# One 512-column matmul for the two parts of the tokens in an MLP's first layer

## The chip, the core and the metric

The kernel runs on one core of one Trainium2 chip. TensorE (PE) multiplies, VectorE (DVE), ScalarE (ACT) and GpSimd (POOL) do the rest, and SyncE (SP) issues most DMAs. The metric is the device time of one execution in microseconds (us). A program is run several times, and the median is compared.

## What is computed

A block of 2048 tokens with 640 channels: a layer norm with shift and scale from a condition, a long convolution with gates, a second layer norm, and an MLP with squared Relu, added to the stream with a gate. The change lies in the MLP:

```python
def _B_ref(x, w1, b1, w2, b2):
    h = jnp.einsum("bsd,df->bsf", x, w1) + b1     # 640 -> 1728
    zero = jnp.zeros_like(h)
    r = jnp.where(h > zero, h, zero)
    h = r * r
    out = jnp.einsum("bsf,fd->bsd", h, w2) + b2   # 1728 -> 640
    return out

h = _layernorm(x, axis=-1) * (1 + cb) + sb
x = x + gb * _B_ref(h, B_w1, B_b1, B_w2, B_b2)
```

## The kernel before

The first half of the time (up to about 290 us) goes to the convolution, which the change does not touch. The MLP follows. It works on eight chunks of `CH` = 256 tokens (`n` = 0 to 7) and, within a chunk, on 14 tiles of the hidden layer (`f` = 0 to 13): thirteen of 128 hidden units and a last one of 64.

Matrices go through PE in the type float32r. To keep the precision, each operand is split in a high part and a low part (the rest): `WI[1, f]` holds both parts of the first layer's weights, `XT[n]` both parts of the chunk's normalized tokens, with shape [128, 2, 5, 256] (part, block of 128 channels, token), and a ring `hring` both parts of the hidden units. A product is then the sum of three: high by high, high by low and low by high.

- `mlp_front(n, f, b)` multiplies block `b` of the five channel blocks. For a full tile these are three matmuls of 256 columns (line 720), all into one PSUM tile `h`; fifteen for the five blocks. The pool of tag "T" gives two such tiles by turns. The tile of 64 units keeps its weights' two parts side by side and has two matmuls for each block (line 711). `mlp_front_first` does the first two tiles of chunk 0 (line 734).
- `mlp_front_end` takes the PSUM tile to SBUF: ACT adds the bias and applies Relu (line 752, tile `mtmp`), POOL squares (line 151, a helper's line). For the tile of 64 units, whose two halves of PSUM hold two sums, it is ACT with the bias (748), VectorE's add (154), ACT's Relu (750) and POOL's square.
- `mlp_split` makes the two parts of the result: ACT copies the high part to `hring` (line 146, a helper's), and VectorE subtracts (line 157).
- `mlp_back(n, f)` is the second layer: 12 matmuls of 320 columns into four PSUM tiles `acc` (line 790), and 8 for the tile of 64 units.
- `mlp_end` multiplies the four sums by the gate on VectorE (line 805), which frees them for the next chunk; `mlp_out` adds the stream, for one half on POOL and for the other on VectorE (line 154), and stores.
- In tiles 8 to 12 of a chunk the next chunk's tokens are made: `prep_xt1` transposes on PE (685) and scales on VectorE (687); `prep_xt2` copies the high part on ACT (146) and subtracts the low part on POOL (157).

The order on each engine is that in which the code is written; `keep_order` pins it. One step `i` of the loop over all (n, f) writes the second layer of the tile three steps back (`MLAG` = 3), the split of the tile one step back, the first layer of this tile, its way out of PSUM, and then what else the step has:

```python
mlp_back(*seq[i - MLAG])       # mlp_end when that was a chunk's last tile
mlp_split(*seq[i - 1])
for b in range(NB):
    mlp_front(*seq[i], b)
mlp_front_end(*seq[i])
```

Of the kernel before, what the change touches and what calls it, by code (L numbers as in the profile page):

```python
# [11 lines left out]
F32 = mybir.dt.float32  # L12
F32R = mybir.dt.float32r
AF = mybir.ActivationFunctionType
ALU = mybir.AluOpType
# [3 lines left out]
P = 128  # L19
NB = D // P  # L20
# [4 lines left out]
CH = 256  # L25
# [67 lines left out]
def ssm_mlp_kernel(  # L93
# [21 lines left out]
    pe, act, dve, pool, sp = nc.tensor, nc.scalar, nc.vector, nc.gpsimd, nc.sync  # L115
# [12 lines left out]
    ps = ctx.enter_context(tc.tile_pool(name="ps", bufs=1, space=bass.MemoryType.PSUM))  # L128
# [21 lines left out]
    def mul(eng, o, a, b):  # L150
        eng.tensor_mul(o, a, b)  # L151

    def add(eng, o, a, b):
        eng.tensor_add(o, a, b)  # L154
# [430 lines left out]
    WI = {}  # L585
# [52 lines left out]
    XT = {}  # L638
# [63 lines left out]
    b1t = sb.tile([P, NF], F32, tag="b1t", name="b1t")  # L702
    accs, hs, rs, hps = {}, {}, {}, {}

    def mlp_front(n, f, b):
        m = P if f < NF - 1 else 64
        if b == 0:
            hps[n, f] = ps.tile([P, CH], F32, tag="T", name=f"h_{n}_{f}", bufs=2)
        if m < P:
            for x in range(2):  # L710
                pe.matmul(  # L711
                    hps[n, f],
                    WI[1, f][:, b],
                    XT[n][:, x, b],
                    start=(b == 0 and x == 0),
                    stop=(b == NB - 1 and x == 1),
                )
            return
        for i, (a, x) in enumerate(((0, 0), (0, 1), (1, 0))):
            pe.matmul(  # L720
                hps[n, f][:m],
                WI[1, f][:, a, b],
                XT[n][:, x, b],
                start=(b == 0 and i == 0),
                stop=(b == NB - 1 and i == 2),
            )
# [15 lines left out]
    def mlp_front_end(n, f):  # L742
        m = P if f < NF - 1 else 64
        r = ML["r"][(n * NF + f) % 3]
        h = hps.pop((n, f))
        if m < P:

            act.activation(r[:m], h[m:], AF.Identity, bias=b1t[:m, f : f + 1])
            add(dve, r[:m], h[:m], r[:m])
            act.activation(r[:m], r[:m], AF.Relu)  # L750
        else:
            act.activation(r[:m], h[:m], AF.Relu, bias=b1t[:m, f : f + 1])  # L752
        mul(pool, r[:m], r[:m], r[:m])
# [463 lines left out]
    for i in range(len(seq) + MLAG):  # L1217
        if i >= MLAG:
            n, f = seq[i - MLAG]
# [7 lines left out]
        if i <= last:  # L1227
            n, f = seq[i]
            if i >= 2:
                for b in range(NB):  # L1230
                    mlp_front(n, f, b)
            mlp_front_end(n, f)
            if n == 0:
                if f >= 8 and f - 8 < NB:
                    prep_xt1(n + 1, f - 8)
                beside(f)
            if n + 1 < NC:
                if f == 3:
                    load_x1(n + 1)
                if n and f == 5:  # L1240
                    stats2(n + 1)
                if n and f == 6:
                    stats2_root(n + 1)
                    stats2_end(n + 1)
                if n == 0 and f in (5, 6):
                    prep_hat(1, f - 5)
                if n and f == 7:
                    prep_hat(n + 1, 0)
                    prep_hat(n + 1, 1)
                if f >= 8 and f - 8 < NB:  # L1250
                    (prep_xt if n else prep_xt2)(n + 1, f - 8)
            if f >= 11 and f < 13:
                residual(n, f - 11, pool)
# [25 lines left out]
```

## Time and profile before

| | us |
|---|---|
| median of 3 runs | 696.17 |
| the three runs | 697.38, 691.37, 696.17 |
| the profiled execution, its own time | 693.38 |
| its span, first to last instruction | 691.6 |

The profiled execution is one more than the three runs. Its span is what the trace covers; the rest of its time lies before the first and after the last instruction. In the trace an engine's row has a line of the kernel (often a helper's), the tile written, an arrow, and the tiles read. "PEld" are the weight loads of PE, which run beside its matmuls.

### The profile page before, as it was taken

What the parts mean: (1) busy time and instruction counts of PE and PEld (TensorE: products, weight loads), DVE (VectorE), ACT (ScalarE), POOL (GpSimd) and SP (SyncE); (2) the same over time, 40 slices, a digit from 0 to 9 for tenths busy, and PEclk for the clock granted to TensorE, in tenths of its full rate; (3) what the DMA queues carried; (4) which work ended last, traced back from release to release, by engine and by line L of the source; (5) the groups of instructions that cost most, each with busy time, mean ns of one, the idle gap of its engine ahead of it and who ended that gap; (6) DMA issues with size and microseconds to landing.
All of it is one profiled execution on the core that took longest, in us unless ns stands there. A gap on an engine that the chain in (4) does not pass through costs nothing.

```text
span 691.6 us, 21100 instructions
## 1 busy us (share of the span) xinstructions
PE 657.0 (95%) x9164; PEld 630.8 (91%) x9164; DVE 335.9 (49%) x601; ACT 330.1 (48%) x688; POOL 311.4 (45%) x390
## 2 busy tenths in 40 slices
PE   6699898889999999999999999999999999999996
PEld 4689798778898888889999999999999999999996
DVE  5267584658886697487532322323332332422313
ACT  4436656767976976466324333333233233233221
POOL 1062165359869789443523514415325325225213
PEclk9999999999999999999999999999999999999999
DMA  9897998889671643466020010100200200200101
GB/s 234 244 270 230 233 265 233 236 204 233 191 221 34 173 148 113 127 199 181 1 77 1 26 52 1 41 37 1 77 1 1 77 1 1 77 1 1 39 1 39
DMA packets 110960, 74.76 MB, mean 108 GB/s; under 512 B 48658, under 2 KB 96146, under 8 KB 110868
## 3 DMA queue, kind: packets, MB, share of 16 engines
q1 hardware_dynamic: 108912, 72.87, 37.2%
q8 instruction: 72, 1.18, 0.7%
q10 hardware_dynamic: 1892, 0.54, 0.4%
q14 instruction: 20, 0.16, 0.1%
q0 software_dynamic: 64, 0.01, 0.0%
HBM read 58.98 MB, written 14.42 MB: 106 GB/s over the span
## 4 chain that ended last, share of the span: by engine, by line
PE 81%; DVE 6%; ACT 5%; DMA 4%; issue 2%; POOL 1%; DVEq 0%; POOLq 0%; ACTq 0%; SPq 0%
PE acc L790 27%; PE h L720 26%; PE qp L464 5%; PE pa L383 4%; PE x L398 4%; PE y L541 4%; PE h L398 3%; DMA wm<-in_w_mod_dram 3%; PE t L530 2%; PE h L711 1%; PE xtp L685 1%; DVE KV L261 1%; ACT wx L146 1%; DVE kacc L261 1%; PE vt L276 1%
## 5 line engine op out<-in xcount | busy, mean ns | idle before, releaser
L151 POOL TENSOR_TENSOR mtmp<-mtmp 128x256 f32<-128x256 f32 x112 | 71.4, 638 | 244.4 <-ACT mtmp L752 236.5
L720 PE MATMUL h<-xt,w_S 128*128 128x256 f32 x1290 | 167.5, 281 | 1.1 <-DVE w_S L157 1.1
L720 PEld LDWEIGHTS h<-xt,w_S 128*128 128x128 f32 x1290 | 161.7, 190 | 1.3 <-DVE w_S L157 1.3
L790 PE MATMUL acc<-w_S,hring 128*128 128x320 f32 x960 | 156.6, 311 | 0.2 <-DVE hring L157 0.2
L157 DVE TENSOR_TENSOR hring<-mtmp,hring 128x256 fp32r<-128x256 f32 x112 | 65.4, 584 | 168.3 <-ACT hring L146 168.3
L790 PEld LDWEIGHTS acc<-w_S,hring 128*128 128x128 f32 x960 | 141.7, 188 | 0.8 <-DVE hring L157 0.7
L752 ACT ACTIVATE mtmp<-h,b1t 128x256 f32<-128x256 f32 x104 | 49.4, 475 | 174.0 <-PE h L720 170.8
L146 ACT ACTIVATE hring<-mtmp 128x256 fp32r<-128x256 f32 x112 | 46.5, 416 | 48.8 <-POOL mtmp L151 47.5
L383 PE MATMUL pa<-wx,p 64*64 64x64 f32 x2560 | 49.3, 228 | 10.8 <-issue 6.1
L383 PEld LDWEIGHTS pa<-wx,p 64*64 64x64 f32 x2560 | 43.9, 141 | 16.8 <-issue 11.3
L146 ACT ACTIVATE a<-pa 128x512 f32<-128x512 f32 x80 | 43.5, 608 | 19.7 <-PE pa L383 19.2
L151 DVE TENSOR_TENSOR wx<-x,wx 128x512 f32<-128x512 f32 x64 | 40.8, 683 | 18.9 <-PE x L398 7.7
L541 PE MATMUL y<-wx,wx 128*64 128x64 f32 x1280 | 43.9, 224 | 2.9 <-ACT wx L146 1.6
L541 PEld LDWEIGHTS y<-wx,wx 128*64 128x64 f32 x1280 | 39.9, 138 | 7.4 <-issue 3.4
L398 PE MATMUL x<-a,gb 128*64 128x128 f32 x640 | 41.6, 274 | 3.3 <-DVE wx L151 2.1
L687 DVE TENSOR_SCALAR we<-xtp,cbs 128x256 f32<-128x256 f32 x35 | 19.0, 543 | 46.8 <-PE xtp L685 46.8
L398 PEld LDWEIGHTS x<-a,gb 128*64 128x64 f32 x640 | 35.9, 137 | 4.9 <-PE h L398 3.0
L154 POOL TENSOR_TENSOR wm<-wm,wm 128x640 f32<-128x640 f32 x20 | 32.1, 1606 | 16.9 <-ACT wm L341 16.5
L261 DVE SCALAR_TENSOR_TENSOR KV<-kt,tap,KV 128x511 f32<-128x511 f32 (+2 forms) x48 | 35.9, 748 | 7.6 <-ACT ktail L146 6.0
L146 ACT ACTIVATE q<-qp 128x512 f32<-128x512 f32 (+1 forms) x40 | 21.3, 584 | 35.4 <-PE qp L464 35.4
L398 PE MATMUL h<-a,gb 128*64 128x128 f32 x512 | 34.0, 275 | 1.5 <-ACT wx L146 1.5
L790 PE MATMUL acc<-w_WX,hring 128*128 128x320 f32 x192 | 31.4, 312 | 0.0
(142 smaller groups left out, 1014.2 us busy)
## 6 DMA issues: line engine op xcount, KB each, us to landing
wm<-in_w_mod_dram SPq DMA_DIRECT2D x25, 320.0 KB, 4.1
KV<-in_A_k_dram SPq DMA_DIRECT2D x20, 256.0 KB, 4.6
KV<-in_A_v_dram SPq DMA_DIRECT2D x20, 256.0 KB, 4.4
p<-in_A_ssm_k_dram SPq DMA_DIRECT2D x20, 256.0 KB, 4.7
p<-kv_d SPq DMA_DIRECT2D x20, 256.0 KB, 4.1
xp<-in_A_q_dram SPq DMA_DIRECT2D x20, 256.0 KB, 4.3
q<-in_A_q_dram SPq DMA_DIRECT2D x15, 320.0 KB, 4.5
out_dram<-x SPq DMA_DIRECT2D x14, 320.0 KB, 2.2
```

What stands on the lines that cost most here:

```text
L146: act.activation(o, i, AF.Copy)
L151: eng.tensor_mul(o, a, b)
L154: eng.tensor_add(o, a, b)
L157: eng.tensor_sub(o, a, b)
L261: dve.scalar_tensor_tensor(o, tk[:, : 512 - t], tap[:, b, t : t + 1], o, op0=ALU.mult, op1=ALU.add)
L383: pe.matmul(t[e][64 * r : 64 * r + 64, g].rearrange("p m d -> p (m d)"), pt[b][l, i, 8 * q + g, :], cw[l, r], start=True, stop=True,)
L398: pe.matmul(t[64 * a : 64 * a + 64, s + r], gb[:, g, r, a], AX[b][i][:, 2 * g + a], start=True, stop=True,)
L464: pe.matmul(t[a][:, u], gi[l, 4 * j + u, r], w[r][l, u % 2], start=(r == 0), stop=(r == 1),)
L541: pe.matmul(y[64 * h : 64 * h + 64, 4 * (g % 2) + i].rearrange("p c l d -> p (c l d)"), tss[g][:, i, 64 * r : 64 * r + 64], ca[:, r, h], s ...
L720: pe.matmul(hps[n, f][:m], WI[1, f][:, a, b], XT[n][:, x, b], start=(b == 0 and i == 0), stop=(b == NB - 1 and i == 2),)
L752: act.activation(r[:m], h[:m], AF.Relu, bias=b1t[:m, f : f + 1])
L790: pe.matmul(acc[2 * s + i], h[:, a, s * P : (s + 1) * P], w[:, y, i * 320 : (i + 1) * 320], start=(f == 0 and ti == 0), stop=(f == NF - 1 ...
```

## The change

For full tiles of chunks 1 to 7, the PSUM tile gets two halves of 256 columns and fills its whole 2 KB per partition. One matmul of 512 columns multiplies the weights' high part with both parts of the tokens, read as two runs of 256 columns that lie 5 x 256 elements apart: high by high goes to half 0, high by low to half 1. A second matmul of 256 columns adds low by high to half 0. For each channel block there are thus two matmuls in place of three. The order within a block is both, low for block 0 and low, both for the others.

Behind it, ACT adds the bias to half 1 as it moves it to SBUF, VectorE adds half 0, and one more VectorE operation takes max(r, 0) and multiplies it by r, which is the squared Relu. POOL's square is gone for these tiles. Chunk 0 and the tiles of 64 units stay as they were.

```diff
     def mlp_front(n, f, b):
         m = P if f < NF - 1 else 64
         if b == 0:
-            hps[n, f] = ps.tile([P, CH], F32, tag="T", name=f"h_{n}_{f}", bufs=2)
+            hps[n, f] = ps.tile(
+                [P, 2, CH] if n and m == P else [P, CH], F32, tag="T", name=f"h_{n}_{f}", bufs=2
+            )
+        if n and m == P:
+
+            h, w = hps[n, f], WI[1, f]
+            both = (h, w[:, 0, b], XT[n][:, :, b])
+            low = (h[:, 0], w[:, 1, b], XT[n][:, 0, b])
+            for x in (both, low) if b == 0 else (low, both):
+                pe.matmul(*x, start=(b == 0 and x is both), stop=(b == NB - 1 and x is both))
+            return
...
+        elif n:
+            act.activation(r, h[:, 1], AF.Identity, bias=b1t[:, f : f + 1])
+            add(dve, r, h[:, 0], r)
+            dve.scalar_tensor_tensor(r, r, 0.0, r, op0=ALU.max, op1=ALU.mult)
+            return
         else:
             act.activation(r[:m], h[:m], AF.Relu, bias=b1t[:m, f : f + 1])
         mul(pool, r[:m], r[:m], r[:m])
```

Lines behind the change have moved: 790 is now 805, and 805 is now 820. The new matmuls are on line 717, the max-times on line 764.

PE's order around the end of chunk 1, before. `h_2_1` is tile 1 of chunk 2, `acc_1_0` to `acc_1_3` are chunk 1's four sums, whose last tile of 64 units comes between two tiles of chunk 2:

```order
L720 MATMUL h_2_1_5964<-xt_2_5728,w_S1_3849 128x256 x15
L790 MATMUL acc_1_0_5517<-w_KV_4901,hring_4976 128x320 x2
L790 MATMUL acc_1_1_5518<-w_KV_4901,hring_4976 128x320 x2
L790 MATMUL acc_1_2_5519<-w_KV_4901,hring_4976 128x320 x2
L790 MATMUL acc_1_3_5520<-w_KV_4901,hring_4976 128x320 x2
L720 MATMUL h_2_2_6000<-xt_2_5728,w_S0_4233 128x256 x15
L790 MATMUL acc_2_0_6018<-w_S1_3849,hring_4976 128x320
```

The second of those fronts and what follows it, on PE, in the changed kernel:

```order
L717 MATMUL h_2_2_5940<-xt_2_5692,w_S0_4233 128x512
L717 MATMUL h_2_2_5940<-xt_2_5692,w_S0_4233 128x256 x2
L717 MATMUL h_2_2_5940<-xt_2_5692,w_S0_4233 128x512
L717 MATMUL h_2_2_5940<-xt_2_5692,w_S0_4233 128x256
L717 MATMUL h_2_2_5940<-xt_2_5692,w_S0_4233 128x512
L717 MATMUL h_2_2_5940<-xt_2_5692,w_S0_4233 128x256
L717 MATMUL h_2_2_5940<-xt_2_5692,w_S0_4233 128x512
L717 MATMUL h_2_2_5940<-xt_2_5692,w_S0_4233 128x256
L717 MATMUL h_2_2_5940<-xt_2_5692,w_S0_4233 128x512
L805 MATMUL acc_2_0_5954<-w_S1_3849,hring_4976 128x320
```

Ten matmuls stand where fifteen stood, and tiles and second layer follow one another as before.

VectorE's order at the same place, before. `hring` is the split, the four rows of line 805 are the products with the gate, and `x1_1` is the stream of chunk 1:

```order
L157 TENSOR_TENSOR hring_4976<-mtmp_4806,hring_4976 64x256
L157 TENSOR_TENSOR hring_4976<-mtmp_4806,hring_4976 128x256
L805 TENSOR_TENSOR mtmp_4806<-acc_1_0_5517,gbrow_4865 128x320
L805 TENSOR_TENSOR mtmp_4806<-acc_1_1_5518,gbrow_4865 128x320
L805 TENSOR_TENSOR mtmp_4806<-acc_1_2_5519,gbrow_4865 128x320
L805 TENSOR_TENSOR mtmp_4806<-acc_1_3_5520,gbrow_4865 128x320
L157 TENSOR_TENSOR hring_4976<-mtmp_4806,hring_4976 128x256
L154 TENSOR_TENSOR x1_1_3020<-mtmp_4806,x1_1_3020 128x640
```

And in the changed kernel:

```order
L157 TENSOR_TENSOR hring_4976<-mtmp_4806,hring_4976 128x256
L154 TENSOR_TENSOR mtmp_4806<-h_2_1_5908,mtmp_4806 128x256
L764 SCALAR_TENSOR_TENSOR mtmp_4806<-mtmp_4806 128x256
L820 TENSOR_TENSOR mtmp_4806<-acc_1_0_5505,gbrow_4865 128x320
L820 TENSOR_TENSOR mtmp_4806<-acc_1_1_5506,gbrow_4865 128x320
L820 TENSOR_TENSOR mtmp_4806<-acc_1_2_5507,gbrow_4865 128x320
L820 TENSOR_TENSOR mtmp_4806<-acc_1_3_5508,gbrow_4865 128x320
L157 TENSOR_TENSOR hring_4976<-mtmp_4806,hring_4976 128x256
L154 TENSOR_TENSOR x1_1_3020<-mtmp_4806,x1_1_3020 128x640
L154 TENSOR_TENSOR mtmp_4806<-h_2_2_5940,mtmp_4806 128x256
L764 SCALAR_TENSOR_TENSOR mtmp_4806<-mtmp_4806 128x256
```

The add and the max-times of tile 1 of chunk 2, which wait for ACT, now stand ahead of the four products of chunk 1, and those of tile 2 stand behind the stream's add.

## The prediction

> **What bounds the kernel now.** I read the page first, for the engine that is busiest, then the busy times by stretch of the span, then the groups by line in the stretch that the change touches, and last the timeline there, which gives the price of one matmul. The page:
>
> ```profile
> span 691.6 us, 21100 instructions
> PE 657.0 (95%) x9164; PEld 630.8 (91%) x9164; DVE 335.9 (49%) x601; ACT 330.1 (48%) x688; POOL 311.4 (45%) x390
> ```
>
> PE is busy for 95% of the span. Busy time by stretch, the columns being PE, PEld, DVE, ACT, POOL, the granted clock, DMA share and GB/s:
>
> ```profile
> 0.00:100.00 100.00, 83.38 (x2020) 75.61 (x2022) 58.31 (x113) 50.27 (x95) 30.64 (x69) 0.98 0.92 244
> 345.00:687.00 342.00, 341.35 (x2607) 341.08 (x2605) 104.41 (x218) 111.40 (x247) 117.28 (x149) 1.00 0.07 26
> 384.10:433.70 49.60, 49.60 (x381) 49.60 (x380) 15.64 (x34) 16.70 (x37) 17.52 (x23) 1.00 0.08 28
> ```
>
> The idle PE time lies at the start, where DMA is busy. The change acts on chunks 1 to 7 of the MLP, which run from about 345 us to the end. There PE is never out of work at full clock, and the other engines are busy for a third of the time. The third row is one chunk. So what a chunk saves on PE comes off the end, as long as the vector work behind it does not become late. The groups of that stretch (after the bar: busy us, mean ns of one; then idle time before it and who ended it):
>
> ```profile
> L720 PE MATMUL h<-xt,w_S 128*128 128x256 f32 x1119 | 145.1, 281 | 0.0
> L790 PE MATMUL acc<-w_S,hring 128*128 128x320 f32 x840 | 136.5, 311 | 0.0
> L151 POOL TENSOR_TENSOR mtmp<-mtmp 128x256 f32<-128x256 f32 x89 | 55.9, 628 | 211.9 <-ACT mtmp L752 211.9
> L157 DVE TENSOR_TENSOR hring<-mtmp,hring 128x256 fp32r<-128x256 f32 x90 | 51.5, 572 | 146.9 <-ACT hring L146 146.9
> L752 ACT ACTIVATE mtmp<-h,b1t 128x256 f32<-128x256 f32 x89 | 42.3, 476 | 160.2 <-PE h L720 160.2
> ```
>
> Neither matmul line idles; ACT, POOL and DVE wait down the chain that starts with PE. The means of 281 and 311 ns are lengths of overlapping instructions and not their spacing. The spacing is in the timeline, start of one row to start of the next, here around the end of chunk 1 and near the end of the kernel (columns: start us, length us, engine, line, tiles, count):
>
> ```profile
> 392.44 1.33 PE L790 MATMUL acc<-w_KV,hring 128*128 128x320 f32 x8
> 392.70 0.48 ACT L752 ACTIVATE mtmp<-h,b1t 128x256 f32<-128x256 f32 x1 [1.92 <-PE h L720]
> 392.93 1.68 DVE L805 TENSOR_TENSOR mtmp<-acc,gbrow 128x320 f32<-128x320 f32 x4 [1.69 <-PE acc L790]
> 393.61 1.95 PE L720 MATMUL h<-xt,w_S 128*128 128x256 f32 x15
> 393.96 1.57 POOL L154 TENSOR_TENSOR x<-mtmp,x 128x640 f32<-128x640 f32 x1
> 394.53 1.28 DVE L157 TENSOR_TENSOR hring<-mtmp,hring 128x256 fp32r<-128x256 f32 x1
> 395.39 1.92 PE L790 MATMUL acc<-w_S,hring 128*128 128x320 f32 x12
> 395.74 0.81 DVE L154 TENSOR_TENSOR x<-mtmp,x 128x640 f32<-128x640 f32 x1
> 397.15 0.27 PE L720 MATMUL h<-xt,w_S 128*128 128x256 f32 x1
> ...
> 680.29 1.36 PE L711 MATMUL h<-xt,w_KV 128*128 128x256 f32 x10
> 681.49 1.93 PE L790 MATMUL acc<-w_WX,hring 128*128 128x320 f32 x12
> ```
>
> Fifteen matmuls of 256 columns take 395.39 - 393.61 = 1.78 us, 118.7 ns each; the ten of L711 take 1.20 us, 120 ns each. Twelve of 320 columns take 397.15 - 395.39 = 1.76 us, 146.7 ns each. From 120 to 146.7 ns is 26.7 ns for 64 columns, 0.417 ns a column. So 256 columns stream for 106.7 ns and 320 for 133.3 ns, and both leave 13.3 ns over: a fixed price for each matmul with its weight load, which is the same for two lengths.
>
> **The change, part by part.**
>
> *Front matmuls.* For each of the 13 full tiles in each of 7 chunks, 91 tiles, fifteen matmuls of 256 columns become five of 512 and five of 256. The columns stay the same: 15 x 256 = 5 x 512 + 5 x 256. Five matmuls and five weight loads go. No row has 512 columns, so it is bounded. From below: columns alone, 512 x 0.417 = 213.3 ns. From above: two of 256 as now, 2 x 118.7 = 237.4 ns. A price above that would need a reason that no row shows, and is a rival below. The line through 256 and 320 columns gives 213.3 + 13.3 = 226.7 ns, which I take because it is nearest to the 320-column row and because the fixed part did not shrink from 256 to 320. Per tile 5 x 13.3 = 66.7 ns go, and 91 x 66.7 ns = 6.1 us. The ends are 91 x 5 x (237.4 - 213.3) ns = 11.0 us saved, and nothing saved. All of it lies on PE, which is the path.
>
> The Trainium skill, page "TensorE: Matmul & The Clock Gate", section "Back-to-back issue gap", gives columns / 2.4 + 2.5 ns for the spacing of warm isolated matmuls. This would make 109 ns of 256 columns and 136 ns of 320, 10 ns under both rows; an estimate by the page for 512 is 215.8 ns, and the sum would be 9.8 us instead of 6.1.
>
> *Bias and Relu on ACT become bias alone.* Both are one pass over 256 columns of PSUM (476 ns, the L752 group above). The first layer's tile of 64 rows has the same bias pass already:
>
> ```profile
> L748 ACT ACTIVATE mtmp<-h,b1t 64x256 f32<-64x256 f32 x7 | 3.3, 474 | 10.8 <-PE h L711 10.8
> L154 DVE TENSOR_TENSOR mtmp<-h,mtmp 64x256 f32<-64x256 f32 x7 | 2.9, 418 | 9.1 <-ACT mtmp L748 9.1
> L261 DVE SCALAR_TENSOR_TENSOR KV<-kt,tap,KV 128x511 f32<-128x511 f32 x16 | 12.0, 748 | 6.4 <-ACT ktail L146 6.0
> ```
>
> So this costs nothing.
>
> *Square on POOL goes, add and max-times on VectorE come.* POOL loses 628 ns a tile (L151 above), off the path. The add is the L154 row, 0.42 us. For the max-times of 256 columns there is no row: its ends are 0.42 us (that same pass) and 0.75 us (the same operation on 511 columns, L261); I take 0.45, since it has the columns of the first. VectorE's busy time in a chunk grows from 15.64 to 15.64 + 13 x 0.87 = 27 us of about 48.7. From ACT's start to the split's end it is 0.48 + 0.42 + 0.45 on the new way against 0.48 + 0.63 on the old, then copy and split as now, so 0.25 us more on a chain that may be late by far: the tile is read by the second layer three tiles later, and two fronts and three backs, 2 x 1.7 + 3 x 1.76 = 8.7 us, lie between, one back less at the last tiles. PE, which covers it, does not run dry. The tile's PSUM buffer comes free after the add instead of after ACT, 0.45 us later, and is wanted again after back, front and back, 5.2 us.
>
> *Who stands behind the new waits on VectorE.* Two things. First, in tiles 8 to 12 the scaling of the next chunk's tokens:
>
> ```profile
> 424.43 0.47 ACT L752 ACTIVATE mtmp<-h,b1t 128x256 f32<-128x256 f32 x1 [2.16 <-PE h L720]
> 424.59 0.54 DVE L687 TENSOR_SCALAR we<-xtp,cbs 128x256 f32<-128x256 f32 x1 [1.68 <-PE xtp L685]
> 425.17 0.42 ACT L146 ACTIVATE xt<-we 128x256 fp32r<-128x256 f32 x1 [0.26 <-DVE we L687]
> 425.66 0.74 POOL L157 TENSOR_TENSOR xt<-we,xt 128x256 fp32r<-128x256 f32 x1
> 426.08 0.60 DVE L157 TENSOR_TENSOR hring<-mtmp,hring 128x256 fp32r<-128x256 f32 x1 [0.94 <-ACT hring L146]
> ```
>
> The scaling now waits for ACT, add and max-times: it starts at 424.43 + 0.47 + 0.42 + 0.45 = 425.8 and not at 424.59, 1.2 us later. Its parts of the tokens are then ready at about 427.6. The last such tile is followed by a back, the 1.2 us front of tile 13, another back and four fifths of a front before its last part is read, over 5 us. Covered, so nothing. Second, the four products with the gate at a chunk's end, which free the second layer's sums (L805 above, at 392.93). They now stand behind add and max-times: ACT ends at 393.18, add at 393.6, max-times at 394.1, and the products end every 0.4 us from 394.6 to 395.8. PE wants the first two sums at about 395.3 and 395.5, the other two 0.9 us later. They are free at 394.6, 395.0, 395.4 and 395.8: at least 0.4 us early, so nothing.
>
> *Sum.* Against the profiled execution, 693.38 us: 693.38 - 6.1 = 687.3. That execution is 2.8 us under the median of the three runs (696.17; 691.37 to 697.38). Of the four times the middle is (693.38 + 696.17) / 2 = 694.8, and I set the forecast there: 694.8 - 6.1 = **688.7 us**.
>
> **The rivals.**
>
> *The fixed price is a weight load that longer matmuls hide.* Then 512 columns cost 213.3 ns, 11.0 us go as at the lower end above, and the time is 683.8. For it: PEld is busy as long as PE. Against it: 320 columns give a load more time than 256 and still pay 13.3 ns. The skill's formula above comes close to this case.
>
> *512 columns cost what two of 256 cost.* The fixed part would then go with the columns and not with the instructions, the gain is nothing, 694.8. Against it is the same pair of rows; it would need a price of 0.46 ns a column, while 64 columns more cost 0.417 each.
>
> *The gate products come late.* VectorE's 1.28 us at 394.53, while POOL adds, shows what an operation on two SBUF operands can cost. Were the max-times that long, the products would end 0.83 us later than worked out, the second sum at 395.8 instead of 395.5: some 0.35 us for each of 7 chunk ends, 2.5 us of the 6.1 given back, 691.2. Against it: POOL's own long add waits for the first two products, so it isn't running then.
>
> *Slower: the operand in two pieces.* The 512 columns are two runs of 256, 5 KB apart, and no front or back row has such an operand. If the step from one run to the next costs more than the 10.7 ns between 226.7 and 237.4, the gain is gone; at 26 ns a matmul costs 253 ns, 5 x 15.6 x 91 = 7.1 us are added, 701.9. Nothing in the profile speaks for it.
>
> **How the numbers follow.** Forecast (4 to 8 us saved) 0.62; hidden weight load 0.15; no gain 0.12; late products 0.05; slower 0.06. A measurement of this kernel can tell about 1%, 7 us, from no change, and the forecast is 0.9%, just under it. The forecast's 0.62 I split into 0.24 over and 0.38 within 1%; the hidden load gives 0.14 over and 0.01 within; no gain and late products 0.16 within and 0.01 slower; the slower case 0.05 slower, 0.01 within. Sums: faster 0.38, same 0.56, slower 0.06. The range goes from 683.5, the hidden load, to 695.5, no gain with a little of the spread of the runs. The slower case and the tails are left out.
>
> **What would show it.** The spacing of the new matmuls: 226.7 ns for 512 columns (213 for the hidden load, 237 for no gain, above that for the two pieces), and fronts of about 1.71 us instead of 1.78. A chunk of 48.7 us instead of 49.6. PE busy throughout 345 us to the end, with no idle time before the second layer that ends with L820's products, and POOL's 128x256 squares gone in chunks 1 to 7. I would be wrong if PE idles at chunk ends, if the 512-column price is off the line, or if a stretch before 345 us, where nothing is changed, differs.

## The result and the profile after

Over 18 runs of each kernel, the changed kernel takes 692.22 us (median; 689.22 to 695.88) and the kernel before 696.09 us (691.37 to 699.74). The ratio is 0.9945, with a 95% interval of 0.9925 to 0.9966: a little faster, and within the 1% that I had called no change. The profiled execution of the changed kernel took 690.64 us, its span is 688.9 us.

The page of the changed kernel begins with the busy time, share and count of each engine:

```profile
span 688.9 us, 20280 instructions
PE 656.3 (95%) x8709; PEld 610.1 (89%) x8709; DVE 409.6 (59%) x783; ACT 326.1 (47%) x688; POOL 255.4 (37%) x299
```

PE has 455 matmuls fewer, which is 91 tiles times 5, and as many weight loads fewer. VectorE has 182 operations more and POOL 91 fewer. The busy times of the same stretch of the MLP, first before and then after the change (columns: PE, PEld, DVE, ACT, POOL, granted clock, DMA share, GB/s):

```profile
345.00:679.00 334.00, 334.00 (x2557) 334.00 (x2556) 100.79 (x211) 109.47 (x243) 113.67 (x144) 1.00 0.08 27
```

```profile
345.00:679.00 334.00, 334.00 (x2134) 313.48 (x2133) 177.70 (x392) 106.42 (x244) 60.85 (x57) 1.00 0.08 26
```

PE still has no gap at full clock. PEld, which was busy all the time, now rests for 20 us: a load takes 0.19 us here (mean of line 717's loads), and a matmul of 512 columns some 0.23 us. VectorE went from 30% to 53%. The timeline around the end of chunk 1 in the changed kernel:

```profile
390.62 0.42 DVE L157 TENSOR_TENSOR hring<-mtmp,hring 128x256 fp32r<-128x256 f32 x1 [0.48 <-ACT hring L146]
392.01 1.33 PE L805 MATMUL acc<-w_KV,hring 128*128 128x320 f32 x8
392.26 0.47 ACT L762 ACTIVATE mtmp<-h,b1t 128x256 f32<-128x256 f32 x1 [1.68 <-PE h L717]
392.77 0.42 DVE L154 TENSOR_TENSOR mtmp<-h,mtmp 128x256 f32<-128x256 f32 x1 [1.73 <-ACT mtmp L762]
393.18 1.93 PE L717 MATMUL h<-xt,w_S 128*128 128x512 f32 x10
393.23 0.43 DVE L764 SCALAR_TENSOR_TENSOR mtmp<-mtmp 128x256 f32<-128x256 f32 x1
393.57 1.68 DVE L820 TENSOR_TENSOR mtmp<-acc,gbrow 128x320 f32<-128x320 f32 x4
394.95 1.92 PE L805 MATMUL acc<-w_S,hring 128*128 128x320 f32 x12
```

A row of merged matmuls carries the shape of its first one; the ten of line 717 are five of 512 and five of 256. They take 394.95 - 393.18 = 1.77 us here. Over all fronts of chunks 1 to 7 that follow a second layer directly, the mean from the first start to the next layer's first start is 1.756 us after and 1.784 us before (where two transposes stand ahead of that layer, up to their start). The forecast was 1.71.

How much the MLP gained as a whole is read from two instructions that both kernels have: ACT's bias pass on the tile of 64 units, in chunk 0 and in chunk 7. Before, and then after (columns: start, length, engine, line):

```profile
336.07 0.47 ACT L748 ACTIVATE mtmp<-h,b1t 64x256 f32<-64x256 f32 x1 [0.77 <-PE h L711]
681.69 0.47 ACT L748 ACTIVATE mtmp<-h,b1t 64x256 f32<-64x256 f32 x1 [1.34 <-PE h L711]
```

```profile
336.09 0.47 ACT L758 ACTIVATE mtmp<-h,b1t 64x256 f32<-64x256 f32 x1 [0.76 <-PE h L721]
679.00 0.47 ACT L758 ACTIVATE mtmp<-h,b1t 64x256 f32<-64x256 f32 x1 [1.12 <-PE h L721]
```

From the one to the other it is 345.62 us before and 342.91 after: 2.71 us saved, 30 ns a tile, where 6.1 us and 67 ns were forecast. These stretches repeat to 0.05 us from trace to trace, so they weigh more in what follows than the medians: that of the kernel before lies at 696.09, 692.93 and 693.57 us in the three comparisons of this document. I call them the MLP stretch.

### The profile page after: what moved, and what is told of

Read it like the earlier page. It is cut to its first block, busy times and chain, and to the rows that moved or that the text cites. A ratio compares the mean times of both kernels' runs of the same rounds, so it can differ in the third digit from the quotient of the medians.

```text
span 688.9 us, 20280 instructions
## 1 busy us (share of the span) xinstructions
PE 656.3 (95%) x8709; PEld 610.1 (89%) x8709; DVE 409.6 (59%) x783; ACT 326.1 (47%) x688; POOL 255.4 (37%) x299
## 4 chain that ended last, share of the span: by engine, by line
PE 84%; DVE 5%; DMA 4%; ACT 4%; issue 2%; POOL 0%; SPq 0%; DVEq 0%; ACTq 0%; POOLq 0%
PE acc L805 27%; PE h L717 23%; PE pa L383 5%; PE qp L464 5%; PE x L398 5%; PE y L541 4%; PE h L398 4%; PE h L730 2%; PE t L530 2%; PE h L721 1%; DMA kv_d<-KV 1%; DMA p<-kv_d 1%; PE xtp L685 1%; DVE KV L261 1%; PE kt L239 1%
## 5 line engine op out<-in xcount | busy, mean ns | idle before, releaser
L717 PE MATMUL h<-xt,w_S 128*128 128x512 f32 (+1 forms) x770 | 147.6, 339 | 0.0
L805 PEld LDWEIGHTS acc<-w_S,hring 128*128 128x128 f32 x960 | 144.8, 188 | 2.8 <-DVE hring L157 0.7
L717 PEld LDWEIGHTS h<-xt,w_S 128*128 128x128 f32 x770 | 120.2, 189 | 13.5
L157 DVE TENSOR_TENSOR hring<-mtmp,hring 128x256 fp32r<-128x256 f32 x112 | 67.8, 606 | 68.5 <-ACT hring L146 68.5
L157 POOL TENSOR_TENSOR xt<-we,xt 128x256 fp32r<-128x256 f32 x35 | 27.4, 784 | 200.6 <-ACT xt L146 200.6
L154 DVE TENSOR_TENSOR mtmp<-h,mtmp 128x256 f32<-128x256 f32 (+1 forms) x99 | 41.9, 423 | 97.4 <-ACT mtmp L762 94.1
L762 ACT ACTIVATE mtmp<-h,b1t 128x256 f32<-128x256 f32 x91 | 43.1, 474 | 114.0 <-PE h L717 114.0
L764 DVE SCALAR_TENSOR_TENSOR mtmp<-mtmp 128x256 f32<-128x256 f32 x91 | 39.6, 435 | 3.1
L146 ACT ACTIVATE xt<-we 128x256 fp32r<-128x256 f32 x37 | 15.3, 416 | 43.4 <-DVE we L687 43.4
```

Of the source, the lines that this page charges most:

```text
L146: act.activation(o, i, AF.Copy)
L157: eng.tensor_sub(o, a, b)
L717: pe.matmul(*x, start=(b == 0 and x is both), stop=(b == NB - 1 and x is both))
L762: act.activation(r, h[:, 1], AF.Identity, bias=b1t[:, f : f + 1])
L764: dve.scalar_tensor_tensor(r, r, 0.0, r, op0=ALU.max, op1=ALU.mult)
L805: pe.matmul(acc[2 * s + i], h[:, a, s * P : (s + 1) * P], w[:, y, i * 320 : (i + 1) * 320], start=(f == 0 and ti == 0), stop=(f == NF - 1 ...
```

## The experiments

The question was why a front saves 28 to 30 ns and not 67. The single starts of line 717 show it first. In the order of the tile the matmuls take 231, 117, 120, 233, 117, 237, 119, 235, 117, 234 ns (medians over the fronts of chunks 1 to 7). The short ones take what they took; the long ones take 231 to 237 ns and not 226.7. Two theories: the step between the two runs of memory costs 7 ns ("step"), or there is no fixed price and a column costs 0.457 ns ("columns").

**One run of memory.** The tokens' two parts lie side by side for each channel block; all readers and writers follow.

```diff
-            XT[n] = sb.tile([P, 2, NB, CH], F32R, tag=f"XP{(n + 1) % 2}", name=f"xt_{n}")
+            XT[n] = sb.tile([P, NB, 2, CH], F32R, tag=f"XP{(n + 1) % 2}", name=f"xt_{n}")
...
-            both = (h, w[:, 0, b], XT[n][:, :, b])
...
+            both = (h, w[:, 0, b], XT[n][:, b])
...
```

> The changed kernel with the tokens' two parts of a channel block side by side, so that the 512 columns of the long matmul are one run of memory. In the changed kernel a front of ten takes 1.756 us and a chunk 49.14 us; the long matmuls take 231 to 237 ns where 226.7 were forecast. Theory 'step' (a fixed 13.3 ns for each matmul, and some 7 ns more for the step between the two runs): long matmuls fall to 226.7 ns, the front to 1.72 us, the chunk to 48.7 us. Theory 'columns' (about 0.457 ns a column whatever the length, no fixed part): nothing changes, 49.14 us a chunk within 0.1.

Measured, the two bias passes:

```profile
338.22 0.47 ACT L758 ACTIVATE mtmp<-h,b1t 64x256 f32<-64x256 f32 x1 [0.76 <-PE h L721]
681.13 0.47 ACT L758 ACTIVATE mtmp<-h,b1t 64x256 f32<-64x256 f32 x1 [1.12 <-PE h L721]
```

The MLP stretch is 342.91 us, as with the change, and a front 1.756 us. The step costs nothing; "step" is out.

**Three short matmuls again, with the new work behind PSUM.** This separates the matmuls from what follows them.

```diff
-            both = (h, w[:, 0, b], XT[n][:, :, b])
-            low = (h[:, 0], w[:, 1, b], XT[n][:, 0, b])
-            for x in (both, low) if b == 0 else (low, both):
-                pe.matmul(*x, start=(b == 0 and x is both), stop=(b == NB - 1 and x is both))
+            for i, (a, x) in enumerate(((0, 0), (0, 1), (1, 0))):
+                pe.matmul(
+                    h[:, x],
+                    w[:, a, b],
+                    XT[n][:, x, b],
+                    start=(b == 0 and i == 0),
+                    stop=(b == NB - 1 and i == 2),
+                )
```

> The changed kernel with three matmuls of 256 columns again for each block, into the two halves of the new PSUM tile; bias on ACT, add and max-times on VectorE as in the change. It separates the matmuls from what follows them. If the work behind PSUM costs PE nothing (both theories): a front of fifteen takes 1.78 us and a chunk 49.53 us as before the change. If the new VectorE work costs something that the trace of the change hides: above 49.6 us.

```profile
334.89 0.47 ACT L762 ACTIVATE mtmp<-h,b1t 64x256 f32<-64x256 f32 x1 [0.78 <-PE h L725]
680.52 0.47 ACT L762 ACTIVATE mtmp<-h,b1t 64x256 f32<-64x256 f32 x1 [1.11 <-PE h L725]
```

The MLP stretch is 345.63 us, that of the kernel before, and a front 1.784. So bias, add and max-times on their new engines cost PE nothing, and the 2.7 us belong to the matmuls.

**The spacing by itself.** A program of nothing but rows of 64 matmuls (`REP` is 64), with PE as its only busy engine; `x` are the columns that are multiplied, `w` two weights of 128 columns:

```python
def series(name, moving, weights, start=None):
    ...
    for i in range(REP):
        m = moving(i)
        ...
        pe.matmul(o, weights(i), m, start=first, stop=last)
...
two = lambda i: w[:, i % 2]
...
series("Hpieces", lambda i: x[:, 0:4:3, 0:256], two)
...
series("Lmixed", lambda i: x[:, 0, 0 : 256 if i % 2 else 512], two)
```

> Only rows of 64 matmuls on random data; nothing of the reference is computed and the output is zeros. Rows A to G: float32r moving operands of 128, 192, 256, 320, 384, 448 and 512 columns in one run, two weights by turns; H: 512 columns in two runs, I: the same in one run read as two; J and K: 512 and 256 columns with the same weights each time; L: 512 and 256 by turns; M and N: bfloat16 with 256 and 512 columns; O: 512 columns from changing places. Theory 'step': 256, 320 and 512 columns in one run take 120, 146.7 and 226.7 ns, and H takes about 234. Theory 'columns': from 320 columns on the time is 0.457 ns a column, 146.7 for 320, 175 for 384, 205 for 448 and 234 for 512, H and I like G; 256 columns take 117 to 120. If the rate belongs to float32r, N takes 213 to 216 ns.

The timeline of PE; start of one row to start of the next, divided by 64, is the spacing:

```profile
26.75 7.26 PE L54 MATMUL sAabc<-x,w 128*128 128x128 f32 x64
33.84 7.34 PE L54 MATMUL sBabc<-x,w 128*128 128x192 f32 x64
41.02 7.86 PE L54 MATMUL sCabc<-x,w 128*128 128x256 f32 x64
48.71 9.55 PE L54 MATMUL sDabc<-x,w 128*128 128x320 f32 x64
58.10 11.26 PE L54 MATMUL sEabc<-x,w 128*128 128x384 f32 x64
69.20 13.38 PE L54 MATMUL sFabc<-x,w 128*128 128x448 f32 x64
82.42 14.71 PE L54 MATMUL sGabc<-x,w 128*128 128x512 f32 x64
96.97 14.67 PE L54 MATMUL sHpieces<-x,w 128*128 128x512 f32 x64
111.48 14.67 PE L54 MATMUL sInear<-x,w 128*128 128x512 f32 x64
125.99 14.67 PE L54 MATMUL sJsamew<-x,w 128*128 128x512 f32 x64
140.49 7.84 PE L54 MATMUL sKsamewshort<-x,w 128*128 128x256 f32 x64
148.17 11.47 PE L54 MATMUL sLmixed<-x,w 128*128 128x512 f32 x64
159.48 7.16 PE L54 MATMUL sMbhalf<-xb,wb 128*128 128x256 bf16 x64
166.48 13.98 PE L54 MATMUL sNbfull<-xb,wb 128*128 128x512 bf16 x62
```

192 columns take 112 ns, 256 take 120.2, 320 take 146.7, 384 take 173.4, 448 take 206.6, and 512 take 226.7 (rows H, I, J; row G, 227.3, has a start that is told below). "Columns" is out as well: in rows of their own kind 256, 320, 384 and 512 columns all leave 13.3 ns beside 0.417 ns a column, as the forecast had it (448 leave 20). Two pieces (H) and repeated weights (J) change nothing. What does not fit is row L: 512 and 256 by turns take (159.48 - 148.17) / 64 = 176.7 ns on average, and half of 226.7 + 120 is 173.3. A pair costs some 7 ns more than its two members cost in rows of their own. The kernel alternates in this way. With bfloat16, 256 columns take 109.4 ns (row M) and 512 take 216 (row N, by its single starts), so most of the 13.3 ns goes with float32r operands.

**The order of long and short ones.** Row G told of a second possibility: in its single starts the first nine matmuls after the 448-column row take 235, 233, 236, 224, 231, 236, 228, 233, 231 ns before they come to 227. So either turns of long and short are dear ("turns"), or any change of length is, until a row has settled ("settling"). A second program repeats the kernel's pattern, twelve of 320 columns and then a front, with other fronts:

```python
L, M, T = 512, 256, 320
...
pattern("Ashort", [M] * 15)
pattern("Bturns", [L, M, M, L, M, L, M, L, M, L])
pattern("Cgroup", [L] * 5 + [M] * 5)
...
pattern("Elong", [L] * 7 + [M])
```

> Only rows of matmuls on random data again; nothing of the reference is computed and the output is zeros. Patterns A to F repeat eight times twelve matmuls of 320 columns and then a front of 3840 columns: A fifteen of 256, B the change's order (512, 256, 256, 512, 256, 512, 256, 512, 256, 512), C five of 512 and then five of 256, D in pairs, E seven of 512 and one of 256, F ten of 384. Theory 'turns' (a long matmul beside a short one costs more than in a row of its own kind, 233 instead of 226.7 ns): A 1.78, B 1.76, C 1.72 to 1.73, D between. Theory 'settling' (after any change of length the first half dozen cost some 6 ns more): C like B, 1.75 to 1.76, and E 1.75 instead of 1.71. G to J: 64 each of 320, 512, 256 and 512 columns; by 'settling' the first six or so of H and J take 231 to 236 ns, by 'turns' only the first. K and L: 256 and 512 columns with weights of 64 columns; if the fixed 13.3 ns is the weight load, they fall towards 109 and 216; if it belongs to float32r, they stay at 120 and 226.7. M: 512 and 256 by turns with weights of 64 columns, N the same in bfloat16: if the price of the turns comes from the weight load, it is gone in both.

One repetition each of A, B, C and E, with the start of the 320-column row that follows, and the rows with weights of 64 columns:

```profile
27.18 1.96 PE L73 MATMUL frontAshort<-x,w 128*128 128x256 f32 x15
28.98 1.92 PE L67 MATMUL backAshort<-x,w 128*128 128x320 f32 x12
...
55.66 1.91 PE L73 MATMUL frontBturns<-x,w 128*128 128x512 f32 x10
57.41 1.93 PE L67 MATMUL backBturns<-x,w 128*128 128x320 f32 x12
...
83.77 1.91 PE L73 MATMUL frontCgroup<-x,w 128*128 128x512 f32 x10
85.52 1.92 PE L67 MATMUL backCgroup<-x,w 128*128 128x320 f32 x12
...
139.95 1.89 PE L73 MATMUL frontElong<-x,w 128*128 128x512 f32 x8
141.68 1.92 PE L67 MATMUL backElong<-x,w 128*128 128x320 f32 x12
...
240.42 7.42 PE L54 MATMUL sKhalfw<-x,w 128*64 128x256 f32 x64
247.68 14.88 PE L54 MATMUL sLhalfw<-x,w 128*64 128x512 f32 x64
262.40 11.06 PE L54 MATMUL sMmix<-x,w 128*64 128x512 f32 x64
273.30 10.57 PE L54 MATMUL sNmixb<-xb,wb 128*128 128x512 bf16 x62
```

The change's order (B) and the grouped one (C) both take 1.75 us, and the seven long ones of E with their short one 1.73, where settled rows would give 1.71. Pairs (D) take 1.742 and 1.756 by turns, and ten of 384 (F) 1.76, where settled rows would give 1.73. The single starts of C are 231, 236, 228, 232, 231 for the long ones, and in the row H of this program, 512 columns after a row of 320, the same five numbers come first, to 1 ns, and then 227 throughout. That is "settling": after a change of length the first five long matmuls cost 1 to 9 ns more each, and a front has only five. Row J, 512 after 256, does the same. The length need not even change: row O of the first program, 512 float32r columns after 512 of bfloat16, spaces its matmuls, behind a first gap of 420 ns, by 231, 231, 235, 229, 232, 231 and then 227.

These rows are no exact copy of the kernel: A takes 1.798 us where the kernel's front of fifteen takes 1.784, so that B saves 47 ns on A and the change 28 on its front. The reason was not found.

With weights of 64 columns the short matmul falls to 113.4 ns (K) but the long one rises to 230.0 (L) and never settles: its single starts go on between 224 and 235 ns. By turns they cost 170.3 on average (M), a little less than the mean of K and L, 171.7, and in bfloat16 turns of 512 and 256 take 216 and 109 ns (N, single starts), which are the prices of the first program's bfloat16 rows. So the extra price of turns was seen only with float32r and weights of 128 columns, as the expectation had it for the case that it comes from the load of the weights. How the load makes it is not shown. K falls half of the way to 109 and L rises, which neither side of their expectation had.

**Grouped in the kernel.** The tile's five long matmuls first, then the five short ones.

```diff
+            if b:
+                return
...
+            for b in range(NB):
+                pe.matmul(h, w[:, 0, b], XT[n][:, :, b], start=(b == 0), stop=False)
+            for b in range(NB):
+                pe.matmul(h[:, 0], w[:, 1, b], XT[n][:, 0, b], start=False, stop=(b == NB - 1))
```

> The changed kernel with each tile's matmuls in another order: the five of 512 columns, then the five of 256. Theory 'turns': the front falls from 1.756 to 1.73 us or less and the chunk from 49.14 to 48.8 or less. Theory 'settling': no change, 49.1 us. The time by 'turns' is some 5 us under the kernel before, by 'settling' 2.7 us.

Two neighbouring fronts of that kernel and its two bias passes:

```profile
499.98 1.31 PE L717 MATMUL h<-xt,w_S 128*128 128x512 f32 x5
501.13 0.75 PE L719 MATMUL h<-xt,w_S 128*128 128x256 f32 x5
501.73 1.92 PE L807 MATMUL acc<-w_S,hring 128*128 128x320 f32 x12
```

```profile
334.63 0.47 ACT L760 ACTIVATE mtmp<-h,b1t 64x256 f32<-64x256 f32 x1 [0.78 <-PE h L723]
676.33 0.47 ACT L760 ACTIVATE mtmp<-h,b1t 64x256 f32<-64x256 f32 x1 [1.11 <-PE h L723]
```

Five long ones take 1.15 us, 230 ns each, and five short ones 0.60, 120 each; over all fronts the mean is 1.741 us. The MLP stretch is 341.70 us, 3.9 less than before and 1.2 less than with the change. Both theories are half right here: the front falls, but not to the 1.73 of "turns". Grouped, the long ones come close to the settled price within the five (230, 231, 231, 228, 227, medians), which the program of rows alone did not show. This is the best version tried. Its ratio to the kernel before is 0.9946 (0.9913 to 0.9978), which cannot be told from the change's 0.9945; that it is 1.2 us better is told by the traces alone.

**POOL's square back.** Long matmuls, but ACT's Relu and POOL's square behind VectorE's add.

```diff
-            dve.scalar_tensor_tensor(r, r, 0.0, r, op0=ALU.max, op1=ALU.mult)
-            return
+            act.activation(r, r, AF.Relu)
```

> The long matmuls of the change, but behind VectorE's add an ACT pass with Relu and POOL's square as before. If all of the gain comes from the matmuls: a chunk of 49.14 us, as with the change. If freeing POOL was part of it: between 49.14 and 49.53.

```profile
335.63 0.47 ACT L758 ACTIVATE mtmp<-h,b1t 64x256 f32<-64x256 f32 x1 [0.76 <-PE h L721]
678.54 0.47 ACT L758 ACTIVATE mtmp<-h,b1t 64x256 f32<-64x256 f32 x1 [0.44 <-PE h L721]
```

342.91 us, the same as the change. Freeing POOL is worth nothing here.

**The size of the difference in time.** The medians say 3.9 us and the traces 2.7. To see whether the work behind PSUM held the rest, the three short matmuls were timed.

> The three short matmuls with the new work behind PSUM once more, now timed. The traces tell 2.7 us for the matmuls of the change, the medians of 18 runs 3.9. If the work behind PSUM is free, this is the same as before: ratio 1.000 within its interval. If it brings the difference, the ratio is about 0.998.

The ratio was 1.0045 (1.0017 to 1.0072), slower than before, which neither expectation had. Its trace has the MLP stretch of the kernel before (345.63 us). So the comparison itself was tried, on another chip, with the kernel before against itself and two kernels a second time.

> The kernel before, unchanged, compared with itself. It tells what the comparison of medians calls a difference where there is none. If its interval is to be trusted to 0.3%, the ratio is within 0.997 to 1.003; if programs or loadings carry an offset of their own in the first 200 us, it can lie outside, and the ratio of 1.0045 of the three short matmuls needs no cause in the MLP.

> The changed kernel again, timed beside the kernel before on this chip. By the traces the MLP is 2.7 us shorter: ratio 0.996. If the 3.9 us of the medians were the true size: 0.9945.

> Three short matmuls with the new work behind PSUM, timed a second time. If the work behind PSUM costs time that the trace of the MLP doesn't show, the ratio is 1.0045 again; if not, 1.000, or no further from it than the kernel before is from itself.

The kernel before against itself gave 1.000 (0.998 to 1.002), the three short matmuls 0.9993 (0.997 to 1.0017), and the change 0.9966 (0.994 to 0.9992). The MLP stretches of these traces were 345.57, 345.62 and 342.91 us. The start of the MLP, behind code that is the same in all kernels, is what moves: the first bias pass stood at 332.28 us in the one trace of the kernel before and at 336.07 in the other. So the 1.0045 did not come again, and 2.7 us (a ratio of 0.9961) lies within both intervals of the change. What made the one comparison differ was not found; the traces cover only profiled executions.

## Why the prediction was right, and where not

*The bound.* Right. PE is busy throughout the MLP before and after, and what the fronts save comes off the end: 28 ns times 91 fronts is 2.5 us of the stretch's 2.7. The rest is too small to place: in these two traces it lies in the 30 second layers behind a transpose (1.841 us instead of 1.846) and in the fronts of 64 units (1.189 instead of 1.196), but in the second trace of the kernel before these took 1.844 and 1.186.

*The front matmuls.* This is the term that was mis-sized: 6.1 us forecast, 2.7 measured. Two parts of it were off. First, the 13.3 ns were measured between rows of one length and then charged to five long matmuls that stand beside short ones. Settled, 512 columns do take 226.7 ns; in the kernel they take 231 to 237. That is 23 ns of the missing 39: the front takes 1.756 us where 5 x 226.7 + 5 x 120 = 1.733. Grouping gives 15 of the 23 back, so most of them belong to the turns of long and short; that the rest is the settling behind the second layer's row is likely from rows C and H, and not shown by itself. What in PE makes either stays open. Second, the fifteen short ones were priced by the row of ten (120 ns) although the row of fifteen beside it had 118.7: 1.800 us taken for a front that takes 1.784, which is the other 16 ns. By the prediction's own sign, a 512-column price off the line, it was wrong here.

*The Trainium skill's formula* (page "TensorE: Matmul & The Clock Gate", section "Back-to-back issue gap"). Columns / 2.4 + 2.5 ns agrees with the bfloat16 rows: 109.4 ns measured for 256 columns and 109.2 by the formula, 216 and 215.8 for 512. For float32r no row of any run reached it: 226.7 ns at best for 512 columns. The 9.8 us that the prediction worked out by it set the formula's price of 512 columns against two measured ones of 256; with the formula on both sides each matmul left out saves 2.5 ns, an estimate of 1.1 us in all.

*The work behind PSUM.* Right at each place. Add and max-times take 0.42 and 0.43 us (0.42 and 0.45 taken). VectorE is busy for 26.4 us of a chunk (27 taken). The gate products begin 1.31 us after ACT's start at a chunk's end, 1.40 by the working, and PE wants their first sum 0.9 us after that product's end. Nothing waits, which the three short matmuls with the new work show: the stretch of the kernel before to 0.01 us. The scaling of the next chunk's tokens does start later:

```profile
423.75 0.47 ACT L762 ACTIVATE mtmp<-h,b1t 128x256 f32<-128x256 f32 x1 [1.13 <-PE h L717]
424.26 0.42 DVE L154 TENSOR_TENSOR mtmp<-h,mtmp 128x256 f32<-128x256 f32 x1 [0.85 <-ACT mtmp L762]
424.71 0.43 DVE L764 SCALAR_TENSOR_TENSOR mtmp<-mtmp 128x256 f32<-128x256 f32 x1
425.06 0.54 DVE L687 TENSOR_SCALAR we<-xtp,cbs 128x256 f32<-128x256 f32 x1
```

1.31 us after ACT's start instead of 0.16: 1.15 us later where 1.2 were taken, and covered.

*The rivals.* The hidden weight load is out: 512 columns keep the fixed part. "No gain" was nearer to the truth than I had given it credit for, though for another reason than a price by columns. The late products did not come. The operand in two pieces is out by two runs, the one-run layout and row H.

*The time.* A good part of this is luck. 688.7 us was forecast, 692.22 measured; the range of 683.5 to 695.5 holds it. "Within 1%" had the largest chance, 0.56, and is what came. The miss of 3.5 us is the sum of three: 3.4 for the mis-sized term, 1.3 because the centre of 694.8 lay that much under the later median of the kernel before, and 1.2 the other way, by which the medians stand further apart than the traces; that the last two nearly cancel is chance. The saving itself, 2.7 us by the traces and 3.9 by these medians, lies under the 4 to 8 us that had a chance of 0.62, and the range holds the time because its upper end was set by "no gain". The sign of a stretch ahead of 345 us that differs can tell nothing: the first bias pass stands at 336.07 us before and 336.09 after, but the two traces of the kernel before lie 3.8 us apart there.

## What to carry to other kernels

Fewer, longer matmuls save the fixed price of each one left out, but settled rows tell too much of it: here they promised 67 ns a tile, rows in the new code's own pattern 47, and the kernel gave 28. So take the price from the pattern, and look for it in the kernel. If lengths must mix, put those of one length together; in this kernel that gave another 15 ns a tile in the traces. And where executions differ by more than the gain, measure the stretch between two instructions that both kernels have.

## What the runs showed of the hardware beyond this

- The spacing of float32r matmuls is not a straight line in the columns: 192 columns cost as much as 128 (112 and 111 ns), and 448 cost 206.6 ns, 20 over their 186.7 of columns, where 384 and 512 are 13.3 over.
- For 512 columns of float32r it takes some matmuls until the spacing is steady: five after 320 columns (231, 236, 228, 232, 231 and then 227 ns) and after 256, nine after 448. For 384 after 320 it took none in the first program (175, 174, 175, 173 ns) and five in the second (175, 177, 185, 176, 182 and then 173).
- A subtraction of 256 columns on VectorE takes 0.42 us alone, 0.60 beside POOL's subtraction and 1.28 beside POOL's long add, as rows of the prediction and the first row of the timeline after show. In both cases it ends 0.28 us after POOL's operation: 394.53 + 1.28 against 393.96 + 1.57, and 426.08 + 0.60 against 425.66 + 0.74. The same 0.28 us comes wherever POOL began first from 345 us on, 39 times in the kernel before and 37 in the changed one.
